# Top-k attention feeding an expert layer on one core: scores moved ahead of the transposes, a fourth score buffer, block pieces kept away from a unit's outputs, one branch in place of two

## Chip, core and metric

The kernel runs on one core of one Trainium2 chip. The metric is device microseconds of one execution; the value of a kernel is the median over its runs. All arithmetic is float32.

## What is computed

The reference is top-k attention, followed by an expert layer in which every token goes to one expert.

```python
# q, k, v: 8 batches, 8 heads, 576 tokens, 64 per head
scores = (q @ k.T) / sqrt(64)
kth    = the 32nd largest score of each row
scores = where(scores >= kth, scores, -1e9)
attn   = exp(scores - max) ; attn /= attn.sum(-1) + 1e-9
x      = (attn @ v)                    # laid out as 4608 tokens x 512
logits = x @ w_gate                    # 8 experts
expert = argmax(logits) ; gate = softmax(logits)[expert]
y      = relu(x @ w1[expert]) @ w2[expert]     # 512 -> 1024 -> 512
out    = gate * y
```

## The kernel before

**Attention.** Two heads make one *unit*: 8 batches of 4 units. A unit has 9 tiles of 128 query rows, handled in 5 *groups*: four pairs of tiles and one single tile (which holds the last 64 rows of both heads). So there are 160 groups, 20 to a batch. A group passes through these steps:

- `scores` (L225): TensorE multiplies queries by keys into `sc` in PSUM; ScalarE copies it to the SBUF tile `s` (L230). `s` has 3 buffers, `sc` has 2 tiles.
- `fold` (L237, L238): VectorE takes maximum and minimum of the two halves of each row.
- `search` (L260 to L281): VectorE finds the 32nd largest value of each row in four rounds of MAX8 and MATCH_REPLACE8. The fold of the next group is put just before the fourth round (`between`), so VectorE, which works in order, waits there if the next group's `s` is late. GpSimd makes the bias `low` from the threshold (L283).
- `depths` (L295): ScalarE makes a mask from `s` and `low`. `weights` (L305, L308): GpSimd subtracts it from `s`, and ScalarE takes the exponential.
- `transposed` (L321, L329): TensorE transposes the weights; ScalarE copies them out (L324, L332).

When the last group of a unit has been transposed, `outputs` (L350 to L366) multiplies by the values, transposes back and forms the gate logits; `scaled` (L379 to L388, GpSimd) divides by the row sums, first the logits `lt` into `lg`, then `x`. After the fourth unit of a batch `route` (from L395, VectorE) finds every token's expert, `scatter` (L438) writes the token rows to memory sorted by expert, and `table` lists the *blocks* that are now complete.

**Expert blocks.** A block is 128 rows of one expert. `load_block` reads its rows and 4 MB of weights; `block` does the two products on TensorE (L548 and L558, after a transpose at L533) with ScalarE steps between (L535, L553, L562), and GpSimd writes the rows out with an indirect DMA (L563). A block is cut into 16 *pieces*, each four L548 products or one L558 product (a float32 product shows as two records). Pieces of blocks that are ready are dealt out among the attention groups of later batches at a steady rate; of the 40 blocks that always run, 24 go there, 2 are kept back for the end of the attention and 14 follow it.

**Order.** The main loop of iteration i emits: search(i) with the fold of i+1 inside it; the transposes of group i-1; the scores of group i+2; depths and weights of group i; if group i-1 closed a unit, its outputs; then the pieces due. A scheduler then sets the order on each engine, and each engine works strictly in that order. `add_manual_dep(..., AFTER)` ties one instruction behind another in the order, without a semaphore. Block matmuls are tied that way behind the last score matmul (`pinned`, `k.last_pe`); the transposes are not.

**Rare parts.** After the blocks come two branches on values that the kernel has computed: one runs spare blocks if more than the 14 are needed, the other redoes everything exactly if a row of the fast search was doubtful. With these inputs neither is taken.

Of the kernel before, what the change touches and what calls it, by code (L numbers as in the profile page):

```python
# [9 lines left out]
F32 = mybir.dt.float32  # L10
I32 = mybir.dt.int32
AF = mybir.ActivationFunctionType
ALU = mybir.AluOpType
# [30 lines left out]
def kernel(  # L44
# [36 lines left out]
    nc = tc.nc  # L81
    B, U, P, _, S = qk.shape
    N, Dm = out.shape
    E = moe_w_gate.shape[1]
# [76 lines left out]
    run = const.tile([P, E], F32, name="run")  # L161
    nc.vector.tensor_copy(run, e_at)
    rest_i = const.tile([1, 1], I32, name="rest_i")
    done = const.tile([1, E], F32, name="done")
    nc.vector.memset(done, 0.0)

# [48 lines left out]
    def scores(n, tiles):  # L215
        todo = []
        got = []
        for i in tiles:
            ps = k.ps_s.tile([P, 2, SM], F32, name="sc")
            todo += [(ps, h, rows, cols) for h, rows, cols in parts(i)]  # L220
            got.append(ps)
        for j in range(2):
            for ps, h, rows, cols in todo:
                d = slice(h * D, (h + 1) * D)
                k.last_pe = nc.tensor.matmul(  # L225
                    ps[rows, j, 0:HF], n.q[d, cols], n.k[d, j * HF:(j + 1) * HF], start=True, stop=True
                ).ins
        s = k.att.tile([P, 2, 2, HF], F32, name="s", bufs=2 if k.exact else 3)
        for m, ps in enumerate(got):
            nc.scalar.copy(s[:, m, :, :], ps[:, :, 0:HF])  # L230
        return s

    def fold(tiles, s):
# [57 lines left out]
    def depths(tiles, s, low):  # L291

        w = k.att.tile([P, 2, S], F32, name="w", bufs=3)
        for m in range(len(tiles)):
            nc.scalar.activation(  # L295
                w[:, m, :], s[:, m, :, :].rearrange("p j k -> p (j k)"), AF.Relu,
                scale=-STEEP, bias=low[:, m:m + 1],
            )
        return w

    def weights(n, tiles, s, w, nbias):
# [11 lines left out]
    def transposed(n, tiles, w):  # L313
        pair = len(tiles) == 2
        if tiles[0] == 0:
            n.wT = k.wtp.tile([P, NC, 2, S], F32, name="wT")
            n.wTt = k.wtp.tile([ST, 2, S], F32, name="wTt")
        for m, i in enumerate(tiles):
            pm = bank("wTm")
            for c in range(NC):  # L320
                nc.tensor.transpose(pm[:, c * P:(c + 1) * P], w[:, m, c * P:(c + 1) * P], ident)  # L321
            pm4 = pm[:, :].rearrange("p (c q) -> p c q", c=NC)
            if pair:
                nc.scalar.copy(n.wT[:, :, m, tiles[0] * P:(tiles[0] + 1) * P], pm4)  # L324
            else:
                nc.scalar.copy(n.wT[:, :, :, SM:S], pm4.rearrange("p c (h q) -> p c h q", h=2))  # L326
        pt = bank("wTl")
        for m in range(len(tiles)):
            nc.tensor.transpose(pt[0:ST, m * P:(m + 1) * P], w[:, m, SM:S], ident)  # L329
        if pair:  # L330
            q = slice(tiles[0] * P, (tiles[0] + 1) * P)
            nc.scalar.copy(n.wTt[:, :, q], pt[0:ST, 0:2 * P].rearrange("p (h q) -> p h q", h=2))  # L332
        else:
            nc.scalar.copy(n.wTt[:, :, SM:S], pt[0:ST, 0:P].rearrange("p (h q) -> p h q", h=2))
# [41 lines left out]
    def scaled(n, x, lg):  # L376

        rzb = rz_of[n.u % 2][:, :].rearrange("p (t h) -> p t h", h=2)
        put = nc.gpsimd.tensor_tensor(n.lt, n.lt, _inner(rzb, E), op=ALU.mult).ins  # L379
        if not k.exact:  # L380
            tc.add_manual_dep(put, k.last_pool.name, AFTER)
        if n.u:
            nc.gpsimd.tensor_tensor(lg, lg, n.lt[:, :, 0, :], op=ALU.add)
            nc.gpsimd.tensor_tensor(lg, lg, n.lt[:, :, 1, :], op=ALU.add)
        else:
            nc.gpsimd.tensor_tensor(lg, n.lt[:, :, 0, :], n.lt[:, :, 1, :], op=ALU.add)
        xu = x[:, :, n.u * P:(n.u + 1) * P].rearrange("p t (h d) -> p t h d", h=2)
        put = nc.gpsimd.tensor_tensor(xu, xu, _inner(rzb, D), op=ALU.mult).ins  # L388
        if not k.exact:
            tc.add_manual_dep(put, k.last_pool.name, AFTER)  # L390
# [71 lines left out]
    def table(n, last):  # L462

        sm = k.small
        lo = sm.tile([1, E], F32, name="lo")
        nc.vector.tensor_tensor(lo, run[0:1, :], e_at[0:1, :], op=ALU.subtract)
        if last:
            nc.vector.tensor_scalar_add(lo, lo, float(P - 1))
        ci = sm.tile([1, E], I32, name="ci")
        nc.vector.tensor_copy(ci, lo)  # L470
        nc.vector.tensor_single_scalar(ci, ci, 7, op=ALU.arith_shift_right)
        full = sm.tile([1, E], F32, name="full")
        nc.vector.tensor_copy(full, ci)
        left = sm.tile([1, E], F32, name="left")
        nc.vector.tensor_tensor(left, full, done, op=ALU.subtract)
        upto = sm.tile([1, E], F32, name="upto")
        nc.vector.tensor_tensor_scan(upto, ones[0:1, 0:E], left, 0.0, op0=ALU.mult, op1=ALU.add)
        past = sm.tile([1, NSLOT, E - 1], F32, name="past")
        nc.vector.tensor_tensor(
            past[:, 0:n, :], _inner(slots[:, 0:n], E - 1), _ins(upto[:, 0:E - 1], 1, n), op=ALU.is_ge  # L480
        )
        slot_f = sm.tile([1, 2, NSLOT], F32, name="slot_f")
        nc.vector.tensor_reduce(slot_f[:, 0, 0:n], past[:, 0:n, :], axis=AX.X, op=ALU.add)
        step = sm.tile([1, E - 1], F32, name="step")
        nc.vector.tensor_tensor(step, done[:, 1:E], full[:, 0:E - 1], op=ALU.subtract)
        nc.vector.tensor_scalar_add(step, step, float(CAP // P))
        nc.vector.tensor_tensor(past[:, 0:n, :], past[:, 0:n, :], _ins(step[:, :], 1, n), op=ALU.mult)
        nc.vector.tensor_reduce(slot_f[:, 1, 0:n], past[:, 0:n, :], axis=AX.X, op=ALU.add)
        nc.vector.scalar_tensor_tensor(
            out=slot_f[:, 1, 0:n], in0=slot_f[:, 1, 0:n], scalar=done[:, 0:1], in1=slots[:, 0:n],  # L490
            op0=ALU.add, op1=ALU.add,
        )
        none = sm.tile([1, NSLOT], F32, name="none")
        nc.vector.tensor_scalar(none[:, 0:n], slots[:, 0:n], upto[:, E - 1:E], float(EMPTY), ALU.is_ge, ALU.mult)
        nc.vector.tensor_tensor(slot_f[:, 1, 0:n], slot_f[:, 1, 0:n], none[:, 0:n], op=ALU.max)
        nc.vector.tensor_scalar_min(slot_f[:, 1, 0:n], slot_f[:, 1, 0:n], float(EMPTY))
        slot_i = sm.tile([1, 2, NSLOT], I32, name="slot_i")
        nc.vector.tensor_copy(slot_i[:, :, 0:n], slot_f[:, :, 0:n])
        if last:
            nc.vector.tensor_copy(rest_i, upto[:, E - 1:E])  # L500
        else:
            nc.vector.tensor_tensor(upto, left, upto, op=ALU.subtract)
            nc.vector.tensor_scalar(upto, upto, float(n), 0.0, ALU.add, ALU.max)
            nc.vector.tensor_tensor(upto, upto, left, op=ALU.min)
            nc.vector.tensor_tensor(done, done, upto, op=ALU.add)
        return slot_i
# [67 lines left out]
    with ExitStack() as st:  # L574
# [81 lines left out]
        def later():  # L656
            if late is not None:
                next(late, None)
# [11 lines left out]
        def ready(i):  # L670
            b, u, g = work[i]
            if g == groups[0]:
                open_unit(unit_of[b, u])
            return scores(unit_of[b, u], g)
# [5 lines left out]
        for i, (b, u, g) in enumerate(work):  # L680
# [5 lines left out]

            low, nbias = search(n, g, s_of[i], hl_of.pop(i), between)
            later()
            if last is not None:
                transpose_last(last)  # L690
            if i + 2 < len(work):
                s_of[i + 2] = ready(i + 2)
            w = depths(g, s_of[i], low)
            weights(n, g, s_of.pop(i), w, nbias)
            later()
# [9 lines left out]
            if b == B - 1 and at >= ARRIVED:  # L705
                room -= KEEP
                credit = room / (per_batch - at)
            n_now = max(0, min(int(credit + 1e-6), room))
            credit = min(credit - n_now, rate)
            pieces(n_now)  # L710
        transpose_last(last)
        close(last)
# [6 lines left out]
        pieces(ALWAYS * PIECES)  # L719
        for _ in current:  # L720
            pass
        more = nc.values_load(rest_i[0:1, 0:1], min_val=0, max_val=LAST)  # L722
        with tc.If(more > ALWAYS):
            for slot in spare:
                for _ in block(load_block(*slot)):
                    pass

        any_p = k.small.tile([P, 1], F32, name="any_p")
        nc.vector.tensor_reduce(any_p, doubt, axis=AX.X, op=ALU.max)
# [2 lines left out]
        nc.tensor.matmul(pd[0:1, 0:1], any_p, ones[:, 0:1], start=True, stop=True)  # L732
        any_i = const.tile([1, 1], I32, name="any_i")
        nc.vector.tensor_copy(any_i, pd[0:1, 0:1])

    again = nc.values_load(any_i[0:1, 0:1], min_val=0, max_val=P)
    with tc.If(again > 0):
        with ExitStack() as st:
            keep = st.enter_context(tc.tile_pool(name="keep", bufs=1))
            open_pools(st, True)  # L740
# [77 lines left out]
```

## Time and profile before

| | us |
|---|---|
| median of 3 runs | 1656.35 (1655.14 to 1656.78) |
| profiled execution, its own time | 1664.02 |
| its span, first to last instruction | 1662.2 |
| TensorE busy | 1457.5 |
| VectorE busy | 1237.7 |
| ScalarE busy | 934.2 |
| GpSimd busy | 666.3 |

The profiled execution has three stages. Up to about 1399 us there is attention, and from the third batch on blocks beside it; VectorE and TensorE are both nearly full there. From 1399 to 1649 us only blocks run. The last 12 us hold the two branches and the program's end. The `mx` instruction at L395, the first of a batch's routing, marks the end of each batch: it starts at 191.1, 360.0, 525.2, 697.9, 878.1, 1047.4, 1232.9 and 1398.6 us. These marks are the stages used below: batch 0 is 22 to 191 us, batch 1 is 191 to 360 us, and so on to batch 7.

"Granted clock" is the share of full speed that TensorE's throttle gave it. A wait "A <- B" is idle time of A that ended when B finished.

### The profile page before, as it was taken

What the parts mean: (1) busy time and instruction counts of PE and PEld (TensorE: products, weight loads), DVE (VectorE), ACT (ScalarE), POOL (GpSimd) and SP (SyncE); (2) the same over time, 40 slices, a digit from 0 to 9 for tenths busy, and PEclk for the clock granted to TensorE, in tenths of its full rate; (3) what the DMA queues carried; (4) which work ended last, traced back from release to release, by engine and by line L of the source; (5) the groups of instructions that cost most, each with busy time, mean ns of one, the idle gap of its engine ahead of it and who ended that gap; (6) DMA issues with size and microseconds to landing.
All of it is one profiled execution on the core that took longest, in us unless ns stands there. A gap on an engine that the chain in (4) does not pass through costs nothing. (4 is left out here: it accounts for less than half of the span.)

```text
span 1662.2 us, 24985 instructions
## 1 busy us (share of the span) xinstructions
PE 1457.5 (88%) x7874; PEld 924.2 (56%) x7874; DVE 1237.7 (74%) x4258; ACT 934.2 (56%) x1937; POOL 666.3 (40%) x993
## 2 busy tenths in 40 slices
PE   5777878788999989898999999899999987899996
PEld 3444434445555555555666555556655554577764
DVE  8999979999899898889888999977889994000000
ACT  4666646665676676656665777656566763111111
POOL 3444544545444544444345544544345543000000
PEclk8666656668999999989999999989999988999998
DMA  1000010007232533245441633353334333788883
GB/s 59 23 23 23 34 40 23 23 23 266 82 142 78 208 142 120 91 159 202 171 151 54 241 137 136 113 189 136 137 128 160 136 115 143 285 308 304 295 319 130
DMA packets 102191, 230.69 MB, mean 139 GB/s; under 512 B 5150, under 2 KB 25630, under 8 KB 102048
## 3 DMA queue, kind: packets, MB, share of 16 engines
q1 hardware_dynamic: 95904, 210.06, 35.2%
q0 software_dynamic: 6144, 18.92, 3.1%
q8 instruction: 66, 1.08, 0.3%
q14 instruction: 77, 0.63, 0.1%
HBM read 207.68 MB, written 22.33 MB: 138 GB/s over the span
## 5 line engine op out<-in xcount | busy, mean ns | idle before, releaser
L305 POOL TENSOR_TENSOR w<-s,w 128x576 f32<-128x576 f32 x288 | 424.2, 1487 | 302.3 <-ACT w L295 301.8
L260 DVE MAX8 tops<-scr 128x8 f32<-128x288 f32 x864 | 353.8, 445 | 0.9
L225 PE MATMUL sc<-qkb 64*128 64x288 f32 (+1 forms) x1280 | 346.0, 506 | 7.3 <-DMA qkb<-in_qk_dram 5.9
L548 PEld LDWEIGHTS ph<-xTs,w 128*128 128x128 f32 x2560 | 305.3, 198 | 24.2 <-issue 21.9
L548 PE MATMUL ph<-xTs,w 128*128 128x128 f32 x2560 | 315.6, 283 | 1.3 <-ACT xTs L535 1.3
L558 PE MATMUL py<-w,hT 128*128 128x512 f32 x640 | 310.4, 629 | 5.4 <-ACT hT L553 5.3
L308 ACT ACTIVATE w<-w,nbias 128x576 f32<-128x576 f32 x288 | 223.3, 776 | 158.4 <-POOL w L305 156.9
L321 PE MATMUL wTm<-ident,w 128*128 128x128 f32 x1152 | 197.4, 312 | 115.7 <-ACT w L308 113.7
L295 ACT ACTIVATE w<-s,low 128x576 f32<-128x576 f32 x288 | 215.6, 776 | 98.4 <-POOL low L283 98.2
L321 PEld LDWEIGHTS wTm<-ident,w 128*128 128x128 f32 x1152 | 147.8, 158 | 200.5 <-ACT w L308 169.2
L268 DVE MATCH_REPLACE8 scr<-tops,scr 128x288 f32<-128x288 f32 x576 | 250.1, 440 | 0.0
L237 DVE TENSOR_TENSOR hl<-s 128x576 f32<-128x576 f32 (+1 forms) x160 | 130.1, 813 | 129.4 <-ACT s L230 129.0
L225 PEld LDWEIGHTS sc<-qkb 64*128 64x128 f32 (+1 forms) x1280 | 158.4, 204 | 102.6 <-issue 56.7
L558 PEld LDWEIGHTS py<-w,hT 128*128 128x128 f32 x640 | 121.9, 201 | 143.3 <-issue 133.8
L230 ACT COPY s<-sc 128x576 f32<-128x576 f32 x288 | 173.4, 636 | 34.6 <-PE sc L225 25.6
L324 ACT COPY wT<-wTm 128x512 f32<-128x512 f32 x256 | 140.5, 586 | 42.3 <-PE wTm L321 42.2
L350 PE MATMUL po<-wT,vb 128*64 128x288 f32 x1024 | 157.2, 455 | 1.4 <-ACT wT L326 1.4
L563 POOL DMA_INDIRECT out_dram<-y,xg x40 | 40.7, 1017 | 242.3 <-ACT y L562 220.4
L262 POOL TENSOR_SCALAR nbias<-tops 128x2 f32<-128x2 f32 (+1 forms) x160 | 34.9, 218 | 246.4 <-DVE thr L281 139.9
L238 DVE TENSOR_TENSOR hl<-s 128x576 f32<-128x576 f32 (+1 forms) x160 | 129.6, 810 | 0.0
L268 DVE MATCH_REPLACE8 scr<-tops,hl 128x288 f32<-128x288 f32 x288 | 125.3, 440 | 0.1
L260 DVE MAX8 tops<-hl 128x8 f32<-128x288 f32 x288 | 124.8, 441 | 0.0
(119 smaller groups left out, 1244.2 us busy)
## 6 DMA issues: line engine op xcount, KB each, us to landing
w<-in_moe_w_dram SPq DMA_DIRECT2D x80, 2048.0 KB, 11.2
qkb<-in_qk_dram SPq DMA_DIRECT2D x32, 576.0 KB, 3.9
xg<-x_rows SPq DMA_DIRECT2D x40, 257.0 KB, 2.7
vb<-in_v_dram SPq DMA_DIRECT2D x32, 320.0 KB, 3.2
x_rows<-blank SPq DMA_DIRECT2D x9, 257.0 KB, 4.5
x_rows<-x,posi POOLq DMA_INDIRECT x40, 3.0
out_dram<-y,xg POOLq DMA_INDIRECT x40, 2.8
wg<-in_moe_w_gate_dram SPq DMA_DIRECT2D x1, 16.0 KB, 1.9
```

Of the source, the lines that this page charges most:

```text
L225: k.last_pe = nc.tensor.matmul(ps[rows, j, 0:HF], n.q[d, cols], n.k[d, j * HF:(j + 1) * HF], start=True, stop=True).ins
L230: nc.scalar.copy(s[:, m, :, :], ps[:, :, 0:HF])
L260: nc.vector.max(out=tops[:, m, r * 8:(r + 1) * 8], in_=src[m])
L268: nc.vector.match_replace(out=scr[:, m, :], in_to_replace=tops[:, m, r * 8:(r + 1) * 8], in_values=src[m], imm_value=NEG,)
L295: nc.scalar.activation(w[:, m, :], s[:, m, :, :].rearrange("p j k -> p (j k)"), AF.Relu, scale=-STEEP, bias=low[:, m:m + 1],)
L305: k.last_pool = nc.gpsimd.tensor_tensor(w[:, m, :], s[:, m, :, :].rearrange("p j k -> p (j k)"), w[:, m, :], op=ALU.subtract).ins
L308: nc.scalar.activation(w[:, m, :], w[:, m, :], AF.Exp, scale=scale, bias=nbias[:, m:m + 1], accum_out=n.z[:, c + m:c + m + 1],)
L321: nc.tensor.transpose(pm[:, c * P:(c + 1) * P], w[:, m, c * P:(c + 1) * P], ident)
L324: nc.scalar.copy(n.wT[:, :, m, tiles[0] * P:(tiles[0] + 1) * P], pm4)
L350: nc.tensor.matmul(po[r, 0:HF], lhsT, rhs, start=(c == 0), stop=(c == KC - 1))
L548: pinned(nc.tensor.matmul(ph[:, f, :], n.w1[:, 0, dt, fc * P:(fc + 1) * P], n.xT[:, dt, :], start=(dt == 0), stop=(dt == DT - 1),))
L558: pinned(nc.tensor.matmul(py, hT[:, f, :], n.w2[:, 0, f, :], start=(f == 0), stop=(f == FT - 1)))
```

## The change

1. In the main loop the scores of group i+2 are emitted before the transposes of group i-1, and the transposes are now pinned behind the last score matmul on TensorE. On ScalarE the mask (`depths`) of a group is tied behind the last score copy.
2. `s` has four buffers in place of three.
3. In an iteration whose group is the first of a unit (the one beside which the previous unit's outputs stand) no pieces are dealt. What was not dealt is carried over: the carry may reach two groups' worth instead of one.
4. In `scaled`, the division of `x` is tied behind the addition of the logits.
5. The two rare parts sit inside one outer branch, on the sum of their two conditions. VectorE computes this sum with two small instructions and a cast; the table of the last batch is kept in a tile of its own so that the inner branch can still read it.

```diff
-        s = k.att.tile([P, 2, 2, HF], F32, name="s", bufs=2 if k.exact else 3)
+        s = k.att.tile([P, 2, 2, HF], F32, name="s", bufs=2 if k.exact else 4)
         for m, ps in enumerate(got):
-            nc.scalar.copy(s[:, m, :, :], ps[:, :, 0:HF])
+            k.last_act = nc.scalar.copy(s[:, m, :, :], ps[:, :, 0:HF]).ins
...
-            nc.scalar.activation(
+            put = nc.scalar.activation(
                 w[:, m, :], s[:, m, :, :].rearrange("p j k -> p (j k)"), AF.Relu,
                 scale=-STEEP, bias=low[:, m:m + 1],
-            )
+            ).ins
+            if not k.exact:
+                tc.add_manual_dep(put, k.last_act.name, AFTER)
...
-                nc.tensor.transpose(pm[:, c * P:(c + 1) * P], w[:, m, c * P:(c + 1) * P], ident)
+                pinned(nc.tensor.transpose(pm[:, c * P:(c + 1) * P], w[:, m, c * P:(c + 1) * P], ident))
...
-            nc.gpsimd.tensor_tensor(lg, lg, n.lt[:, :, 1, :], op=ALU.add)
+            k.last_pool = nc.gpsimd.tensor_tensor(lg, lg, n.lt[:, :, 1, :], op=ALU.add).ins
...
         if last:
             nc.vector.tensor_copy(rest_i, upto[:, E - 1:E])
+            nc.vector.tensor_scalar(rare, upto[:, E - 1:E], float(ALWAYS), None, ALU.is_gt)
...
             low, nbias = search(n, g, s_of[i], hl_of.pop(i), between)
             later()
+            if i + 2 < len(work):
+                s_of[i + 2] = ready(i + 2)
             if last is not None:
                 transpose_last(last)
-            if i + 2 < len(work):
-                s_of[i + 2] = ready(i + 2)
             w = depths(g, s_of[i], low)
...
-            n_now = max(0, min(int(credit + 1e-6), room))
-            credit = min(credit - n_now, rate)
+            n_now = 0 if g == groups[0] else max(0, min(int(credit + 1e-6), room))
+            credit = min(credit - n_now, 2 * rate)
             pieces(n_now)
...
-        more = nc.values_load(rest_i[0:1, 0:1], min_val=0, max_val=LAST)
-        with tc.If(more > ALWAYS):
-            for slot in spare:
-                for _ in block(load_block(*slot)):
-                    pass
...
+        nc.vector.tensor_tensor(rare, rare, pd[0:1, 0:1], op=ALU.add)
+        rare_i = const.tile([1, 1], I32, name="rare_i")
+        nc.vector.tensor_copy(rare_i, rare)
...
+    with ExitStack() as outer:
+        either = nc.values_load(rare_i[0:1, 0:1], min_val=0, max_val=P + 1)
+        outer.enter_context(tc.If(either > 0))
...
+            with tc.If(more > ALWAYS):
...
+        again = nc.values_load(any_i[0:1, 0:1], min_val=0, max_val=P)
+        outer.enter_context(tc.If(again > 0))
```

## Prediction

> **What bounds the kernel now.** First the page: busy shares in 40 slices, then the one wait of VectorE that counts.
>
> ```profile
> PE   5777878788999989898999999899999987899996
> ...
> DVE  8999979999899898889888999977889994000000
> ...
> PEclk8666656668999999989999999989999988999998
> ```
>
> VectorE is nearly full up to 1399 us, TensorE from there to the end. In slices 2 to 9, before any blocks run, TensorE has only 0.64 to 0.70 of its clock (stages below). Next the list of waits, whole span:
>
> ```profile
> DVE hl L237 <- ACT s L230: 129.0, 54, 8.9
> ```
>
> VectorE stands still 129.0 us in 54 places, all at the fold, because the next group's scores have not been copied. Nothing else in its main stage is near. Whether this can be won depends on TensorE, so next the stages by batch (start:end, length, then busy time of TensorE, its weight loads, VectorE, ScalarE, GpSimd, and the clock):
>
> ```profile
> 22.00:191.00 169.00, 134.80 (x593) 75.21 (x593) 161.54 (x529) 113.75 (x238) 78.77 (x117) 0.70 0.09 26
> 191.00:360.00 169.00, 134.27 (x563) 75.04 (x564) 151.51 (x511) 105.57 (x222) 79.05 (x118) 0.64 0.09 30
> 360.00:525.20 165.20, 147.07 (x793) 89.08 (x792) 154.41 (x532) 109.76 (x229) 79.42 (x119) 0.88 0.37 138
> 525.20:697.90 172.70, 156.35 (x903) 98.41 (x904) 151.20 (x533) 114.86 (x240) 80.32 (x121) 0.96 0.38 138
> 697.90:878.00 180.10, 164.10 (x963) 108.63 (x964) 153.50 (x533) 114.40 (x240) 82.10 (x122) 0.93 0.44 159
> 878.00:1047.40 169.40, 159.59 (x925) 99.29 (x924) 154.86 (x534) 114.07 (x241) 82.83 (x122) 0.98 0.39 141
> 1047.40:1232.90 185.50, 169.56 (x963) 112.60 (x960) 154.36 (x533) 113.94 (x240) 81.80 (x122) 0.91 0.43 154
> 1232.90:1398.60 165.70, 146.24 (x826) 91.09 (x824) 136.49 (x459) 102.91 (x217) 76.97 (x109) 0.92 0.38 133
> ```
>
> Batches 0 to 2 are VectorE's: it has 151 to 162 us of work. In batches 3 to 6 TensorE has more (156 to 170 against 151 to 155), so there at most TensorE's own idle time can go. Last, the timeline of one stall in batch 4:
>
> ```profile
> 707.57 5.47 PE L548 MATMUL ph<-xTs,w 128*128 128x128 f32 x24
> ...
> 713.76 1.07 ACT L324 COPY wT<-wTm 128x512 f32<-128x512 f32 x2 [3.50 <-PE wTm L321]
> ...
> 716.32 1.16 ACT L230 COPY s<-sc 128x576 f32<-128x576 f32 x2
> ...
> 717.51 1.46 DVE L237 TENSOR_TENSOR hl<-s 128x576 f32<-128x576 f32 x1 [3.75 <-ACT s L230]
> ```
>
> 24 block matmuls hold TensorE 5.47 us; the transposes come after them, ScalarE stands 3.50 us at their copy, the score copy stands behind that, and VectorE loses 3.75 us.
>
> **Parts 1 and 2, order and fourth buffer.** In the built order of batches 3 to 6 the score copy of group k stood behind the mask of group k-2 in 61 of 80 groups; now it stands behind that of k-3 in 79 of 80. On TensorE the scores of k move from behind the transposes of k-3 (75 of 80) to behind those of k-4 (all 80). Batches 0 and 1 had a distance of 3 to the mask and now have 4. So every copy is one group earlier. A pair costs VectorE about 151.5 / 18 = 8.4 us (batch 1 has 16 pairs and 4 singles, 18 pair-equivalents), a single tile 4.2. No matmul, copy or DMA is added; the 8 score matmul records and 2 copies of a group only change places.
>
> - Batches 0 and 1: waits at the fold after 22 us are 5.9 and 13.1, none longer than 6.1. A lead of 4.2 to 8.4 more covers nearly all: **-16 us**, bounds 0 and -19. VectorE is then late itself: 313 us busy in about 322.
> - Batch 2: waits 9.8, TensorE 147.1 of 165.2. **-7**, bounds 0 and -9.8.
> - Batches 3 to 6: waits 19.8 + 22.1 + 12.6 + 28.4 = 82.9. TensorE is busy 649.6 of 707.7. Its idle waits for the output copy (px, 3.5 + 5.9 + 3.0 + 9.6 = 22.0) and for the transposes' copy (wTl, 8.5 + 3.8 + 4.0 + 1.2 = 17.5) do not depend on VectorE and stay: 649.6 + 39.5 = 689.1, 18.6 less. A little more should come from the clock: block matmuls at L548 took 5.47 / 24 = 0.228 us in the stall above and 7.31 / 64 = 0.114 us after 1600 us, and stalls are where it falls. If 5 of the 650 us go so: **-23**. Bounds: 0 (TensorE gives nothing) and -82.9 (all waits; TensorE would have to run its 650 us of work in 625).
> - Batch 7: waits 11.7 at the fold; TensorE 146.2 of 165.7. **-8**, bounds 0 and -11.7.
>
> The new tie adds a wait: the mask of group j now stands behind the score copy of j+2, hence behind all pieces that follow the transposes of j-2. Behind it on ScalarE queue the exponentials of j, which GpSimd and the transposes of j need. From the end of those scores: copy 0.64, transposes 0.6, two copies out 1.2, mask 0.78, two subtractions 2.8, exponential 0.97, together 7.0 us a pair, less than VectorE's 8.4. So I take it at nothing, and its other end in the rival below.
>
> **Part 3, pieces.** The 384 pieces before the end stay 384; a piece is 7.31 / 8 = 0.91 us. At the outputs 3 or 4 are taken away and follow in the next group, 6 to 8 there, 5.5 to 7.3 us. I take it at nothing because the lead covers one such burst; bounds -6 and +70 (the rival).
>
> About the clock: in batch 1 TensorE waits for weights 27 times, 32.4 us, a mean of 1.2, and gets 0.64. The Trainium skill ("TensorE: Matmul & The Clock Gate", Part 1) has the clock fall only after an idle window of about 3.4 us; by that rule batch 1 would be mostly at full speed and the gaps opened beside the outputs (px waits up to 2.8 us) would be free. By the row they need not be. The sum uses neither.
>
> **Part 4.** The logits are ready before the 1.26 us division of `x` (L388). VectorE waits for them 12.3 us at the last batch, 4.0 and 1.3 at two others. The last one counts: the first block after the kept pair is late by 6.0 us (its xg load). **-1.5**, bounds 0 and -3.8.
>
> **Part 5, branches.** Both skipped branches show on GpSimd's sequencer after the last store is issued:
>
> ```profile
> L723 POOLq INC_SWDGE_SEM  x1: 1788/1788/1788, 1649.8 to 1649.8; - x1
> L737 POOLq INC_SWDGE_SEM  x1: 1757/1757/1757, 1653.0 to 1653.0; - x1
> L813 POOLq DRAIN  x3: 40/107/6611, 1654.8 to 1662.0; - x3
> ```
>
> The second starts with its load at 1651.6 and is over at 1654.8; one branch saves that: **-3**, bounds 0 (the 6.6 us drain ends on something else) and -3.9 (TensorE's own second branch, 3.87). The three new VectorE instructions lie near 1428 us, where VectorE has nothing else. The skill's "Advanced Engine Details and Errata" (Control Flow Timing) gives a compare-and-branch as about 108 ns; by it this part would be worth 0.1 us.
>
> **Sum**: 16 + 7 + 23 + 8 + 1.5 + 3 = 58.5. The profiled execution took 1664.0 us (span 1662.2 and 1.8 around it), 7.7 above the median of 1656.35; 1664.0 - 58.5 = 1605.5, and on the median's scale **1598 us**. The blocks after the attention, 15.1 us each at 14.3 us of TensorE work, do not change.
>
> **Rivals.**
> - *TensorE holds batches 3 to 6 altogether*: its 92% busy is all it can do, and score copies come earlier only to wait elsewhere. Without the 23 and half of batch 7: 58.5 - 27 = 31.5, 1625 us. For it: TensorE's busy time exceeds VectorE's in all four. Against: 12.9 us of its idle time there waits for exponentials, which are VectorE's lateness come back.
> - *Stalls fed one another*: a late score makes late masks, late transposes, an idle TensorE at half clock and later scores. With the loop cut, 60 of the 82.9 go: 1598 - 37 = 1561 us. For it: 0.228 against 0.114 us. Against: batch 5 has 0.98 of the clock and still 12.6 us of waits.
> - *The burst*: slower. The mask tied behind a score copy that is behind 6 to 8 pieces makes ScalarE, and through it VectorE, pay the doubled share: 3.5 pieces, 3.2 us, in some 22 units, 70 us against 58.5, 1668 us. It decides where burst, transposes and scores (7.3 + 1.6 + 2.2 = 11 us) exceed the lead VectorE has gained, between 8.4 and 10 us. For it: the order puts 23 block matmuls ahead of the scores there. Against: outputs and burst are now in separate groups, where 8.4 us of outputs and 3 pieces were together.
> - *No effect on the waits*: if the copies come no earlier in time, 4.5 us remain: 1652 us.
>
> **Numbers.** Forecast 0.52; TensorE's bound 0.20; the loop 0.13; the burst 0.11; no effect 0.04. The forecast's own bounds are 1580 to 1615. The range goes from 1555, just past the loop's 1561, to 1642, halfway from TensorE's case to the burst's: it leaves out the slower cases (0.15) and a little below. This kernel can be told from no change at about 0.2%, 1653 to 1660: faster 0.85, same 0.04, slower 0.11.
>
> **What would show it.** Right: the 129 us at L237 fall under 60; batches 0 and 1 take 158 to 163 us; batches 3 to 6 take 163 to 178 with TensorE at 94% or more; one INC_SWDGE_SEM before the last drain. Wrong: the fold's waits stay above 100, or ScalarE's waits at the mask or the transposes' copies grow by as much, with TensorE's clock below 0.9 in batches 3 to 6.

## The result and the profile after

| | median us | runs |
|---|---|---|
| before | 1656.57 | 4, from 1655.14 to 1657.07 |
| after | 1696.28 | 4, from 1691.43 to 1703.59 |

The ratio is 1.0245, with a 95% interval from 1.0207 to 1.0283: the change makes the kernel slower by some 40 us, where 58 us were forecast to go. The profiled execution after took 1691.43 us (span 1689.5), 27.4 more than that of before; these 27.4 us are what the two traces can explain. The page of after, the same rows:

```profile
PE   6877878788989899889998998899998987899997
...
DVE  8999899989789989998898789997898794000000
...
PEclk7677667767989799999998799989998898999999
```

The picture is the old one: VectorE nearly full to the end of the attention, TensorE after it. The list of waits of VectorE, whole span:

```profile
DVE hl L239 <- ACT s L232: 95.1, 33, 6.7
DVE mx L399 <- POOL lg L388: 34.6, 8, 12.0
```

The fold's wait fell from 129.0 to 95.1 us, so the change does what it says. In return the wait for the logits rose from 20.0 to 34.6, and that for `over` from 4.4 to 10.5. The stages by batch, marked by `mx` as before (start:end, length, then busy time of TensorE, its weight loads, VectorE, ScalarE, GpSimd, and the clock):

```profile
22.00:195.64 173.64, 137.06 (x579) 78.27 (x579) 165.36 (x529) 112.42 (x235) 78.12 (x117) 0.69 0.08 24
195.64:366.07 170.43, 131.80 (x565) 76.01 (x565) 157.68 (x511) 105.86 (x223) 80.78 (x118) 0.69 0.09 29
366.07:536.67 170.60, 153.41 (x850) 99.16 (x852) 154.23 (x533) 113.14 (x235) 82.80 (x121) 0.87 0.38 135
536.67:714.08 177.41, 161.90 (x920) 102.41 (x916) 164.91 (x542) 114.65 (x239) 87.27 (x125) 0.90 0.38 135
714.08:891.76 177.68, 158.91 (x943) 102.95 (x943) 159.16 (x536) 115.35 (x241) 85.67 (x122) 0.97 0.45 159
891.76:1076.13 184.37, 166.72 (x926) 108.61 (x927) 161.35 (x531) 115.67 (x240) 87.38 (x123) 0.87 0.37 131
1076.13:1257.55 181.42, 166.48 (x962) 107.51 (x959) 160.60 (x535) 115.53 (x241) 84.92 (x122) 0.94 0.45 157
1257.55:1426.44 168.89, 142.68 (x765) 88.49 (x765) 132.39 (x448) 101.31 (x212) 78.15 (x107) 0.86 0.36 131
```

The busy time that changed most is the third, VectorE's: it works 323.0 us in batches 0 and 1 (313.0 before) and 646.0 in batches 3 to 6 (614.0 before). The account closes. Batches 0 and 1: waits at the fold 19.0 to 5.2 (-13.8), VectorE's work +10.0, and the waits for the logits at the end of the two batches 7.9 and 7.1 us (1.3 and 4.0 before): +6.0 together. Batches 3 to 6: waits at the fold 82.9 to 58.5 (-24.4), work +32.0, other waits +5.6: +13.2. Batch 2 +5.4, batch 7 +3.2, behind the attention -0.5. Sum +27.3.

VectorE has the same instructions as before but for three; some became longer. The group of `both`, the small minimum that ends a search, is shown first in before, then in after (behind the count: busy us, mean ns, idle us before it):

```profile
L277 DVE TENSOR_TENSOR both<-tops 128x18 f32<-128x18 f32 (+1 forms) x160 | 36.5, 228 | 0.5
```

```profile
L279 DVE TENSOR_TENSOR both<-tops 128x18 f32<-128x18 f32 (+1 forms) x160 | 58.7, 367 | 0.7
```

In after's trace 53 of the 160 overlap a subtraction on GpSimd (L309) and take 0.70 us on average, the others 0.20; in before 20 overlap. The folds do likewise, 1.09 against 0.68 us. Why the subtraction comes at another time now is seen in the timeline. First before, from a threshold (894.56) to its subtraction:

```profile
894.56 0.16 DVE L281 TENSOR_REDUCE thr<-both 128x2 f32<-128x18 f32 x1
894.80 0.22 POOL L283 TENSOR_SCALAR low<-thr 128x2 f32<-128x2 f32 x1 [0.36 <-DVE base L417]
...
897.05 0.80 ACT L295 ACTIVATE w<-s,low 128x576 f32<-128x576 f32 x1
...
897.93 1.41 POOL L305 TENSOR_TENSOR w<-s,w 128x576 f32<-128x576 f32 x1 [2.75 <-ACT w L295]
...
898.66 1.16 ACT L230 COPY s<-sc 128x576 f32<-128x576 f32 x2
```

and the same place in after:

```profile
897.46 0.17 DVE L283 TENSOR_REDUCE thr<-both 128x2 f32<-128x18 f32 x1
897.72 0.22 POOL L285 TENSOR_SCALAR low<-thr 128x2 f32<-128x2 f32 x1 [3.59 <-DVE thr L283]
...
903.44 1.18 ACT L232 COPY s<-sc 128x576 f32<-128x576 f32 x2
...
905.44 0.82 ACT L297 ACTIVATE w<-s,low 128x576 f32<-128x576 f32 x1
...
905.86 1.06 POOL L442 DMA_INDIRECT x_rows<-x,posi  x1 [1.88 <-issue]
...
910.51 0.96 POOL L442 DMA_INDIRECT x_rows<-x,posi  x1 [0.31 <-issue]
...
911.49 1.41 POOL L309 TENSOR_TENSOR w<-s,w 128x576 f32<-128x576 f32 x1
...
912.94 0.78 ACT L312 ACTIVATE w<-w,nbias 128x576 f32<-128x576 f32 x1 [5.77 <-POOL w L309]
...
913.86 1.12 PE L325 MATMUL wTm<-ident,w 128*128 128x128 f32 x4 [3.58 <-ACT w L312]
```

Before, the mask followed `low` after 2.0 us and stood ahead of the score copy. After, it stands behind it: 7.5 us of waiting. Then GpSimd is at row stores (L442), four ahead of the subtraction, which begins 14 us after the threshold in place of 3.2. Over 20 groups of a batch the mean from threshold to subtraction was 1.9 to 4.5 us before and is 5.7 to 9.1 after. The program's end shows what part 5 was to do, one skipped branch ahead of the drain:

```profile
L739 POOLq INC_SWDGE_SEM  x1: 1772/1772/1772, 1680.1 to 1680.1; - x1
```

### The profile page after: what moved, and what is told of

It reads as the page before. It is cut to its first block, busy times and chain, and to the rows that moved or that the text cites. A ratio compares the mean times of both kernels' runs of the same rounds, so it can differ in the third digit from the quotient of the medians.

```text
span 1689.5 us, 24972 instructions
## 1 busy us (share of the span) xinstructions
PE 1468.7 (87%) x7874; PEld 941.1 (56%) x7874; DVE 1276.4 (76%) x4261; ACT 940.5 (56%) x1937; POOL 691.4 (41%) x993
## 5 line engine op out<-in xcount | busy, mean ns | idle before, releaser
L309 POOL TENSOR_TENSOR w<-s,w 128x576 f32<-128x576 f32 x288 | 433.2, 1518 | 463.7 <-ACT w L297 462.9
L312 ACT ACTIVATE w<-w,nbias 128x576 f32<-128x576 f32 x288 | 223.0, 775 | 235.2 <-POOL w L309 235.1
L325 PE MATMUL wTm<-ident,w 128*128 128x128 f32 x1152 | 216.3, 332 | 137.1 <-ACT w L312 128.9
L563 PE MATMUL py<-w,hT 128*128 128x512 f32 x640 | 310.4, 620 | 23.9 <-ACT hT L558 23.3
L553 PE MATMUL ph<-xTs,w 128*128 128x128 f32 x2560 | 324.2, 284 | 5.9 <-ACT xTs L540 5.9
L553 PEld LDWEIGHTS ph<-xTs,w 128*128 128x128 f32 x2560 | 312.1, 200 | 24.5 <-issue 14.8
L325 PEld LDWEIGHTS wTm<-ident,w 128*128 128x128 f32 x1152 | 156.1, 167 | 228.6 <-ACT w L312 181.8
L227 PEld LDWEIGHTS sc<-qkb 64*128 64x128 f32 (+1 forms) x1280 | 168.7, 210 | 129.9 <-issue 65.1
L239 DVE TENSOR_TENSOR hl<-s 128x576 f32<-128x576 f32 (+1 forms) x160 | 135.2, 845 | 95.3 <-ACT s L232 95.1
L563 PEld LDWEIGHTS py<-w,hT 128*128 128x128 f32 x640 | 117.6, 199 | 133.3 <-issue 102.7
L240 DVE TENSOR_TENSOR hl<-s 128x576 f32<-128x576 f32 (+1 forms) x160 | 133.7, 835 | 0.0
L262 DVE MAX8 tops<-hl 128x8 f32<-128x288 f32 x288 | 125.4, 442 | 0.0
L267 DVE MAX8 tops<-hl 128x8 f32<-128x288 f32 x288 | 119.8, 445 | 0.8
```

The source lines that it names most:

```text
L227: k.last_pe = nc.tensor.matmul(ps[rows, j, 0:HF], n.q[d, cols], n.k[d, j * HF:(j + 1) * HF], start=True, stop=True).ins
L262: nc.vector.max(out=tops[:, m, r * 8:(r + 1) * 8], in_=src[m])
L309: k.last_pool = nc.gpsimd.tensor_tensor(w[:, m, :], s[:, m, :, :].rearrange("p j k -> p (j k)"), w[:, m, :], op=ALU.subtract).ins
L312: nc.scalar.activation(w[:, m, :], w[:, m, :], AF.Exp, scale=scale, bias=nbias[:, m:m + 1], accum_out=n.z[:, c + m:c + m + 1],)
L325: pinned(nc.tensor.transpose(pm[:, c * P:(c + 1) * P], w[:, m, c * P:(c + 1) * P], ident))
L553: pinned(nc.tensor.matmul(ph[:, f, :], n.w1[:, 0, dt, fc * P:(fc + 1) * P], n.xT[:, dt, :], start=(dt == 0), stop=(dt == DT - 1),))
```

## The experiments

"Stages" are taken from the threshold instructions (L281 before) of groups 0, 60, 140 and 159 in the profiled execution: batches 0 to 2, 3 to 6, 7, and the rest. "Busy" and "idle" are VectorE's in batches 3 to 6. Each ratio is to runs of the kernel before made beside that experiment, so two kernels are better compared by their ratios than by their medians; the stages come from one execution each.

| kernel | median us | ratio to before | 0-2 | 3-6 | busy | idle | 7 |
|---|---|---|---|---|---|---|---|
| before | 1656.4 | | 492 | 708 | 614 | 94 | 163 |
| only45 | 1657.9 | 1.0000 (0.9975 to 1.0024) | 495 | 701 | 620 | 81 | 161 |
| bufs4 | 1666.1 | 1.0044 (1.0018 to 1.0070) | 505 | 699 | 623 | 76 | 157 |
| order_old_pieces_no_tie | 1676.1 | 1.0090 (1.0066 to 1.0115) | 499 | 706 | 623 | 84 | 170 |
| old_pieces | 1674.9 | 1.0095 (1.0065 to 1.0124) | 500 | 704 | 654 | 50 | 162 |
| no_mask_tie | 1699.8 | 1.0247 (1.0203 to 1.0290) | 502 | 724 | 628 | 96 | 162 |
| the change | 1696.3 | 1.0245 (1.0207 to 1.0283) | 500 | 717 | 641 | 76 | 167 |
| after_spread | 1663.2 | 1.0027 (0.9996 to 1.0058) | 500 | 693 | 636 | 58 | 163 |
| oldp_both1 | 1671.4 | 1.0058 (1.0030 to 1.0086) | 500 | 704 | 626 | 78 | 163 |
| spread_bufs3 | 1677.8 | 1.0119 (1.0087 to 1.0151) | 516 | 690 | 631 | 59 | 161 |
| only45_spread | 1696.5 | 1.0221 (1.0194 to 1.0248) | 493 | 726 | 622 | 104 | 173 |
| old_pieces_halfsub | 1562.6, one run | | 457 | 650 | 606 | 44 | 151 |
| old_pieces_halfsub_dummy | 1591.3, one run | | 471 | 665 | 628 | 37 | 155 |
| only45_halfsub | 1564.1, one run | | 451 | 661 | 597 | 64 | 149 |

**The tie of the mask.** My first theory was the burst rival's path: the tie makes the mask late. The tie alone is taken out of the change:

```diff
-            if not k.exact:
-                tc.add_manual_dep(put, k.last_act.name, AFTER)
```

> The change without one tie: the mask (depths) on ScalarE is no longer tied behind the last score copy; all else as in the change. Theory 'late subtraction': in the changed kernel the mask starts 3 to 7 us after its threshold where it was 0.4 to 2.2, so GpSimd's subtraction falls on VectorE's two-input instructions (the threshold's `both`: 58.7 us busy against 36.5, 53 of 160 overlapping a subtraction against 20) and the logits come late. Without the tie batches 3 to 7 get their early mask back: `both` falls under 48 us, and the time to 1665 to 1680 (batches 0 to 2, which have the same order as in the change, stay about 11 us longer than before). Rival 'burst' (doubled pieces in the second group stall the chain): nothing comes back, 1690 to 1700. Rival 'order on TensorE' (transposes behind the scores): 1690 to 1700 too.

Measured 1699.8 us. In batches 4 to 7 the subtraction again begins 2.1 to 3.0 us after the threshold, and no time is won: in batches 3 to 6 VectorE's work falls by 13 us and its idle time rises by 20. The theory fell; late masks alone are not the loss there. In batches 0 to 2 the masks stay late (6.4 to 8.5 us), so for those this run doesn't tell.

**Part by part.** Part 3 is taken back, then order and ties with it, then the fourth buffer too:

```diff
# old_pieces (the change without part 3)
-            n_now = 0 if g == groups[0] else max(0, min(int(credit + 1e-6), room))
-            credit = min(credit - n_now, 2 * rate)
+            n_now = max(0, min(int(credit + 1e-6), room))
+            credit = min(credit - n_now, rate)
# bufs4: also the old order, no tie, transposes not pinned; only45: also three buffers
```

> The change without part 3: pieces dealt to every group as before, carry of one group; the order, ties, buffers and branch of the change stay. Theory 'late subtraction': the mask stays late, 1685 to 1705. Rival 'burst': the doubled share was what cost, 1640 to 1660.

> The kernel before with only the fourth score buffer, the tie of the division behind the logits and the single branch (parts 2, 4 and 5); old emission order, no mask tie, old pieces. In batches 0 and 1 the built order equals that of the change. Theory 'late subtraction': ScalarE now copies scores one group earlier and so ahead of masks, batches 0 to 2 come out at 173, 170 and 170 us as in the change, the rest as before: 1655 to 1668. Rival (an extra buffer only adds slack, as forecast): batches 0 and 1 get shorter than 169, 1630 to 1645.

> The kernel before with only parts 4 and 5 (the division of x tied behind the logits, one branch in place of two). By the forecast's terms 1.5 and 3 us less: about 1652. Theory 'late subtraction' says the same, since no mask moves. If the logits' tie costs (GpSimd's order is changed in all units), it is 1657 or more.

> The change without the mask tie and without part 3: scores emitted ahead of the transposes, fourth buffer, parts 4 and 5. Against bufs4 (1666) it adds only the order, against old_pieces (1675) it lacks only the tie. Theory 'collision': masks stay early in batches 3 to 7, VectorE busy 155 a batch, 1660 to 1670. If the tie is what removes the waits (old_pieces has 58.5 us of fold waits): fold waits 90 or more here.

The last is the change without part 3 and without the mask's tie. By these ratios, on 1656 us: parts 4 and 5 nothing, the fourth buffer +7 us, the new order +8, the tie +1, part 3 +25. They add up to the +41 because each step starts from the one before. Each is known to about 6 to 8 us: part 3 is clear of that, the fourth buffer and the order (with its pinned transposes) barely, and the tie can't be told from nothing. Without the tie part 3 costs as much: 1.0247 (no_mask_tie) against 1.0090, 26 us. The fourth buffer costs in batches 0 to 2, +10 us; there the subtraction begins 6.4 to 8.5 us after the threshold in bufs4, 3.3 to 4.4 in only45.

**The burst.** Part 3 does two things: bare groups beside the outputs, and doubled shares after them. Only the doubling is taken out:

```diff
# after_spread
-            credit += rate
+            if g != groups[0]:
+                credit += 1.25 * rate
```

> The changed kernel, still with no pieces in the first group of a unit, but the other four groups take 1.25 shares each, so that nothing is carried over and no group gets a double share. Theory 'burst' (part 3 costs by the double share in the second group): most of the 21 us between old_pieces and the change comes back, 1675 to 1682. Rival 'outputs left bare' (part 3 costs because TensorE stands idle and its clock falls beside the outputs): 1690 to 1697.

1663.2 us, 33 under the change. The profiled executions differ by 27 us, 24 of them in batches 3 to 6: the doubled share is what part 3 costs. By which path isn't shown. In batches 3 to 6 VectorE's fold waits fall from 58.4 to 40.2 us, and its work by 6 us; TensorE's busy time falls from 651 to 634 us, at a granted clock of 0.94 in place of 0.92. In after, TensorE's list of waits has a line for the second product, in after_spread almost none:

```profile
PE py L563 <- ACT hT L558: 23.3, 11, 6.9
```

```profile
PE py L563 <- ACT hT L558: 1.7, 3, 1.2
```

It is TensorE waiting for ScalarE's step between the two products of a block. But no_mask_tie, dealt like the change, has only 9.8 us there and is no faster, so this wait is not shown to be the loss.

**Even dealing elsewhere.** The same edit with three buffers, and in the old order without ties:

> The change with three score buffers, and with the pieces dealt evenly: none beside a unit's outputs, but nothing carried over, the other four groups of a unit get 1.25 shares. Theory (the fourth buffer costs 8 to 10 us in batches 0 to 2, the doubled share 20 to 33 us, and even pieces away from the outputs help): batches 0 to 2 about 492 to 495, 3 to 6 about 693 to 700; 1650 to 1657 us, 0 to 0.4% under the kernel before. Rival: with three buffers the score copy waits for its buffer again, fold waits are back at 110 or more, and the time is 1660 or more.

> The kernel before with parts 4 and 5 (1657.9 us) and the even dealing alone, old order, three buffers, no ties: no pieces beside a unit's outputs, 1.25 shares beside each of the other four groups. Theory (the dealing helps whatever the order, since outputs and pieces in one group hold the next scores back): batches 3 to 6 fall from 701 to 685 to 693, 1640 to 1652 us. Rival: the gain of the spread was only the cure of the doubled share; then 1655 to 1661.

Both missed. With the new order three buffers cost 17 us more in batches 0 to 2 (516 against 499.5 in after_spread). In the old order even dealing costs 37 us, and VectorE's idle time in batches 3 to 6 grows from 81 to 104 us. There a group's pieces stand ahead of its transposes, and these ahead of the next scores, so a quarter more pieces may delay both; this reason was not tested. The parts are not a sum: the fourth buffer and the dealing lose in the old surroundings and win beside each other.

**Is VectorE's longer work the bound?** The minimum `both` can be had from a reduction over pairs, which reads one tensor:

```diff
# both1, the main lines; tops is laid out anew so that pair can name the two values side by side
-            nc.vector.tensor_tensor(both[:, m2, :], _back(tops[..]), tops[..], op=ALU.min)
...
+            nc.vector.tensor_reduce(both[:, m2, :], pair, axis=AX.X, op=ALU.min)
...
```

> old_pieces (the change without part 3) with the threshold's `both` made by one reduce over pairs that lie 9 apart in one tile, in place of a two-input minimum; same number of VectorE instructions, same values. Theory 'collision' (two-input VectorE instructions are stretched while GpSimd subtracts; old_pieces has 67.6 us busy in `both`, 57 of 160 overlapping, against 36.5 and 20 before): `both` falls to about 160 x 0.17 = 27 us, VectorE's busy time per batch from 164 to about 159, and the time from 1674.9 to 1640 to 1655, below the kernel before. Rival 'TensorE bound' (VectorE's longer instructions only fill time that TensorE would take anyway): 1670 to 1680, with the gain come back as fold waits.

> The changed kernel as it is, with the one-input `both`. Collision theory: 58.7 us of `both` falls to 27, 10 to 30 us less than the change: 1665 to 1685. Rival 'TensorE bound and the burst': within 5 us of the change's 1696.

> The kernel before with parts 4 and 5 and the one-input `both`. Here `both` costs 42.6 us, 15 above its undisturbed 27, and fold waits 120 us absorb part of it. Collision theory: 1645 to 1655. If the one-input form is itself longer or collides too: 1658 or more.

The group `both` in old_pieces, then in oldp_both1:

```profile
L279 DVE TENSOR_TENSOR both<-tops 128x18 f32<-128x18 f32 (+1 forms) x160 | 67.6, 422 | 0.6
```

```profile
L283 DVE TENSOR_REDUCE both<-tops 128x18 f32<-128x36 f32 (+1 forms) x160 | 28.1, 176 | 0.6
```

39.5 us of this group's work are gone (34 of VectorE's in batches 0 to 6), and 3.5 us of time by the medians, 6 by the ratios, which is within the noise; the wait at the fold came back instead, first old_pieces, then oldp_both1:

```profile
DVE hl L239 <- ACT s L232: 58.5, 32, 5.6
```

```profile
DVE hl L239 <- ACT s L232: 89.6, 43, 5.4
```

In the change the same edit gave 1690.1 us (1.0164, 1.0131 to 1.0197), with only parts 4 and 5 1664.0 (1.0027, 1.0006 to 1.0048). So in old_pieces and in only45 VectorE's work is not the bound. In the change it may be: 14 us less of it in batches 0 to 6 went with 6 us by the medians, 13 by the ratios. The Trainium skill ("SBUF — State Buffer", Who interferes with whom) says that a VectorE instruction with two SBUF inputs contends with a GpSimd instruction that reads SBUF, and that one with a single input, outside its 2-port modes, does not. These rows agree: the minimum takes 0.70 us on average beside a subtraction and 0.20 elsewhere, the reduction 0.174 beside one (58 of 160) and 0.177 elsewhere.

**Is TensorE the bound?** Every second L563 product is left out, so the output of the blocks is incomplete:

```diff
# halfpy
-            pinned(nc.tensor.matmul(py, hT[:, f, :], n.w2[:, 0, f, :], start=(f == 0), stop=(f == FT - 1)))
+            if k.exact or f % 2 == 0:
+                pinned(nc.tensor.matmul(py, hT[:, f, :], n.w2[:, 0, f, :], start=(f == 0), stop=(f >= FT - 2)))
```

> old_pieces with half of the second products of every block left out (4 of 8 matmuls at py; the result is then another), 3.5 us less TensorE work in each of 40 blocks, some 16 us a batch in batches 3 to 6; everything else stays. If TensorE holds batches 3 to 6 (704 us in old_pieces, counted between the thresholds of groups 60 and 140): 650 to 670. If the chain mask, subtraction, exponential, transpose holds them: over 690. If both take turns: between.

> The kernel before with parts 4 and 5 and half of the second products left out, the partner of old_pieces_halfpy. If TensorE holds batches 3 to 6 (700.6 us in only45), they fall to 650 to 670 here too; if the fold's waits hold them, they fall with TensorE's pieces as well, but VectorE's 620 us of work and the waits that have nothing to do with pieces (13 a batch) leave at least 670.

1681.6 and 1643.0 us in one run each. Batches 3 to 6 take 712 us (704 with all products) and 695 (701). The products that are gone were 67 and 70 us of TensorE's time in these batches, but its busy time fell only by 15 and 38 us: the granted clock there fell from 0.96 to 0.90 and from 0.95 to 0.91, and the other matmuls took longer. Still TensorE's idle time rose, from 75 to 98 and from 55 to 87 us, with next to no time won: its amount of work does not set these batches.

**GpSimd's subtraction.** Half of its columns are left out (the exponential of the others sees the mask alone):

```diff
# halfsub
-                w[:, m, :], s[:, m, :, :].rearrange("p j k -> p (j k)"), w[:, m, :], op=ALU.subtract
+                w[:, m, 0:HF], w[:, m, 0:HF], s[:, m, 0, :], op=ALU.subtract
...
-                w[:, m, :], w[:, m, :], AF.Exp, scale=scale, bias=nbias[:, m:m + 1],
+                w[:, m, :], w[:, m, :], AF.Exp, scale=-scale, bias=nbias[:, m:m + 1],
```

> old_pieces with GpSimd's subtraction on half of the columns only (the other half keeps the mask alone, so the result is another): some 0.7 us less for each of 288 subtractions, so 1.4 us less in a pair's chain, and half the time in which GpSimd can stretch VectorE. If the chain mask, subtraction, exponential, transpose holds batches 3 to 6: 704 falls to 670 to 685 and batches 0 to 2 from 500 to 485 to 492. If TensorE holds them: batches 3 to 6 stay over 695, batches 0 to 2 still gain.

> The kernel before with parts 4 and 5 (1657.9 us), but GpSimd subtracts only the first half of each row's columns (the exponential of the other half sees the mask alone, so the output isn't the attention's). Theory: the mask, GpSimd's subtraction and the exponential bind both orders; then about 100 us go here as well, to 1550 to 1575, in batches 0 to 2 (495) and 3 to 6 (701) alike. Rival: in the old order the fold's wait (120 us) bounds and the subtraction binds only the late masks of the new order; then under 40 us go: 1620 or more.

1562.6 and 1564.1 us: 112 and 94 us less, the largest effect of any run, in all batches, and the two orders end within 2 us of each other. The subtraction's time bounds both kernels, as a link between mask and exponential or as VectorE's neighbour. The neighbour counts: in old_pieces_halfsub batches 0 to 6 are 97 us shorter, and VectorE's busy time there is 76 us less; in only45_halfsub it is 83 and 39. To tell its place in the chain from its work beside VectorE, as much scratch work was put back off the chain:

```diff
# halfsub_dummy, for each tile, behind the group's own subtractions
+                put = nc.gpsimd.tensor_tensor(spare_w, s[:, m, 1, :], s[:, m, 0, :], op=ALU.subtract).ins
+                tc.add_manual_dep(put, k.last_pool.name, AFTER)
```

> The change without part 3, GpSimd subtracting only half of the columns (1562.6 us in one run; the other half sees the mask alone, so the output isn't the attention's), and GpSimd doing as many subtractions of the same half size again into a scratch tile that nothing reads, each behind the group's own. Theory A, it was the length of the chain from mask to exponential: the scratch work is off that chain, and the time stays at 1560 to 1590. Theory B, it was GpSimd's work beside VectorE's (longer VectorE instructions, or GpSimd's own queue): the time goes back to 1645 to 1675.

The two groups of subtractions, nearly as long as each other:

```profile
L309 POOL TENSOR_TENSOR w<-w,s 128x288 f32<-128x288 f32 x288 | 252.7, 889 | 303.3 <-ACT w L297 301.3
L319 POOL TENSOR_TENSOR spare_w<-s 128x288 f32<-128x288 f32 x288 | 249.2, 865 | 6.3
```

1591.3 us: GpSimd's extra work took back 29 of the 112 us, and VectorE's busy time in batches 0 to 6 rose by 36; 84 stay won with GpSimd as busy as ever. But VectorE's work in batches 0 to 6 is 40 us below old_pieces there too: a fold beside a subtraction takes 0.93 us on average, 1.11 in old_pieces. The run shows that GpSimd's amount of work is the smaller share; how the 84 divide between the chain and shorter blocking it doesn't show. That 34 us less of VectorE's work gave 3.5 to 6 us in oldp_both1 speaks for the chain, no more.

**A shorter chain with all of the work.** The exponential is taken before the threshold, the mask subtracted from it afterwards, and the transposes' copies keep the positive part; the row sums need a pass of their own. In short:

```diff
# exp_first (on only45) and oldp_exp_first (on old_pieces), in words but for the last two lines
...
+        w = exp(scale * s + nbias)             # ScalarE, ahead of the transposes of the group before
+        s = relu(-STEEP * s + low)             # ScalarE, the mask, in place
+        w = w - s                              # GpSimd
+        spare_w, z = relu(w), its row sums     # ScalarE, 288 passes more
-                nc.scalar.copy(n.wT[..], pm4)
+                nc.scalar.activation(n.wT[..], pm4, AF.Relu)
...
```

> The kernel before with parts 4 and 5 (1657.9 us) with the same attention computed in another order: ScalarE takes the exponential of all scores before the threshold is known, GpSimd subtracts the mask from the exponentials afterwards, and the transposes' copies take the positive part, which drops what the mask made negative. The exponential (0.97 us) is thus no longer between the subtraction and the transposes. The row sums need a pass of their own on ScalarE, 288 more of about 1 us, which only the unit's divisors wait for. If the length of the chain from threshold to transposes binds: half of a subtraction (0.7 us) gave 94 us, of which about a quarter was not length; 0.97 us less gives 60 to 100, 1555 to 1600 us. Rival, ScalarE's queue binds: 288 more instructions, 1.7 us a group, make masks and score copies later, 1650 or more.

> The same edit in the change without part 3 (1674.9 us; scores first, four buffers). By the chain: 1565 to 1610, and the fold's waits under 60 us as there, so that it may be the better of the two. By ScalarE's queue: 1660 or more.

1679.0 us (1.0116, 1.0091 to 1.0141) and 1672.3 (1.0062, 1.0041 to 1.0083). ScalarE took on 156 us (1092.1 busy, 936.5 in old_pieces). Batches 3 to 6 fell by 3 and 13 us, batches 0 to 2 rose by 25 and 23, and GpSimd's wait for the mask in exp_first was 364.3 us, 291.1 in only45. Expected were 60 to 100 us less, or a loss by ScalarE's queue; it may be some of each, and neither theory is shown. No kernel here that computes the whole result is faster than before: after_spread comes nearest of those with the new order, and its interval includes no change.

## Why the prediction was wrong

- **What bounds the kernel: wrong.** VectorE nearly full and its one large wait were read as "time that can be won at the fold". In the runs the wait and VectorE's work trade against each other: 58.5 us of fold waits at 1674.9 (old_pieces), 129.0 at about 1657. A wait shows who is late last in that order of the queues. The lever, half a subtraction for 94 us, is on an engine that is 40% busy, and the list of waits had the row, GpSimd idle for the mask, first before, then after:

```profile
POOL w L305 <- ACT w L295: 301.8, 170, 10.9
```

```profile
POOL w L309 <- ACT w L297: 462.9, 148, 10.9
```

- **Batches 0 and 1, -16; batch 2, -7.** The waits went as said in 0 and 1 (-13.8), and +6.0 came out. The step that failed is that nothing else would grow: VectorE's work (+10.0) and the waits for the logits (+9.7). The logits stand on GpSimd behind the subtraction of the next batch's second group, and at the first of these waits GpSimd stands 10.9 us for that group's late mask. The fourth buffer alone costs 10 us in batches 0 to 2. Batch 2 gained no wait at all (9.8 to 13.1).
- **Batches 3 to 6, -23.** The waits fell by 24.4 and VectorE's work grew by 32.0, so the stage grew by 13.2. TensorE's waits for the output copy (px), taken to stay at 22.0, went too (0.6 in the whole span), and that gave no time either. The bound was not TensorE: it is 90.7% busy, and the stage gets at most 6 us shorter with half of the L563 products gone.
- **The tie "at nothing".** The path of 7.0 us a pair, from the end of the scores to that of the exponential, takes 7.9 to 9.1 us in batches 3 to 6, about VectorE's 8.4: the sum had only work in it and no waiting. From the threshold to the end of the exponential the mean is 9.4 to 12.9 us by batch, 5.9 to 8.2 before. By itself the tie cost about 1 us of time, not to be told from nothing, so here the total held though the working didn't.
- **Part 3 "at nothing".** This is the term that made the kernel slower, the largest loss: 25 us, 33 against an even dealing. The burst rival had the right part (70 us priced), but not the path: without the tie part 3 costs 26 us. The cover that I named, a lead of one group, did not hide it. What path the loss takes stays open.
- **Part 4, -1.5, and part 5, -3.** From the last store's issue to the end of the span there are 9.6 us in place of 12.4, so -2.8, nearly as worked out. Part 4 missed its aim: the last batch's wait for the logits is 12.0 us, 12.3 before. Parts 4 and 5 together are 1.0000 of before, with an interval of 0.25% each way: too small to be seen.
- **The signs I named.** Fold waits fell, but not under 60; ScalarE's waits at the exponential, not at the mask, grew (156.9 to 235.1 us). One sum was off: halfway between 1625 and 1668 us is 1646, not 1642; nothing else was worked out from it.

## What to carry to other kernels

In a loop through several in-order queues, an engine that is nearly full, with one large wait, need not be the bound. Shorten a suspected link (half of its columns) and look at the time before work is moved for it; where work that is taken away comes back as waits, it wasn't the bound. When an instruction moves up in a queue, price what it is moved past, and what that one's successors on other engines will then run beside.

## What the runs showed of the hardware

- A small two-input minimum on VectorE, 0.20 us alone, takes 0.70 on average beside a 1.41 us subtraction on GpSimd, and a fold 1.09 in place of 0.68 (the change's trace); a reduction of one input stays at 0.176 (oldp_both1).
- The same matmuls kept TensorE busy 1484.6 us at a mean granted clock of 0.869 in only45_spread and 1400.8 us at 0.912 in old_pieces_halfsub: a busy time is no fixed amount of work.
